# Making w_out's sums for seven-product pairs two pairs at a time, all in batch 1's first half

## The chip, the cores and the metric

One core of one Trainium2 chip runs the whole program. The core has five engines that are told apart here: TensorE (PE, matrix products; its weight loads are listed as PEld), VectorE (DVE), ScalarE (ACT), GpSimd (POOL) and SyncE (SP), which issues the DMA transfers here. The metric is device microseconds of one execution of the kernel. Three runs of the kernel before took 710.82, 713.46 and 713.57 us.

## The reference

Inputs are q, k, v of 8 batches x 8 heads x 576 rows x 64, packed queries p of 32 rows, a w_in of 512 x 2048 and a w_out of 2048 x 512. Cut to what matters:

```
def sm_attn(qq, kk, vv):
    s = scale * np.matmul(qq, kk.transpose(0, 1, 3, 2))
    s = s - np.max(s, axis=-1, keepdims=True)
    a = np.exp(s)
    a = a / (np.sum(a, axis=-1, keepdims=True) + 1e-09)
    return np.matmul(a, vv)
p_packed = sm_attn(p, k, v)
out = sm_attn(q, p_packed, p_packed)          # 8 x 8 x 576 x 64

x = out, heads put side by side               # 4608 tokens x 512
h = x @ w_in                                  # 4608 x 2048
g = h * np.clip(h + 3.0, 0.0, 6.0) / 6.0
return g @ w_out                              # 4608 x 512
```

The packed result of 32 rows serves as keys and as values of the second attention. Behind the attention stand two large products with a gate between them.

## The kernel before, in words

The work goes batch by batch. Batch 0 has its order written out by hand (a long list of steps) and is not touched. For batches 1 to 7, while the two large products of batch b run, the attention of batch b + 1 is made a piece at a time between them.

A batch's 576 tokens are done in two halves (c = 0 and 1; of 320 and 256 tokens in one order or the other, the odd 64 tokens of two neighbouring batches being joined in an "edge" tile). A half walks over the 2048 columns of w_in in 16 steps of 128 columns, f = 0 to 15. In each step `first_product` (L929) makes h for 128 columns: 12 matmuls a step on the halves `a_hi`, `a_lo` and `m_hi`, `m_lo`, since every float32 operand is split into a high part and a low part and three products (high by high, high by low, low by high) are summed. `m` is w_in already multiplied with the packed keys, so that the second attention's result needn't be formed: u_m, L350, makes it from w_in a quarter (512 columns) at a time, which is why w_in is needed again in every batch. It is kept in DRAM as `w_kept` (written at batch 1's step 0, L1376, four transfers of 1 MB) and fetched back as `w_again` (L1380).

`gate_into` makes the gate: a ReLU on ACT (L940) and a multiply with a minimum on DVE (L941). Then g is split: ACT casts the high part (L946), POOL or DVE subtracts for the low part (L947). The second products (L969) of a step are queued and come two steps later, or, for pairs, one pair later, so that the gate and the split have time.

A single step costs the second product 6 matmuls of 512 columns (two blocks of 128 tokens by three products). A *pair* takes two steps f, f + 1 at once as a 2 x 2 block product with seven instead of eight block products: 21 matmuls of 256 columns in place of 12 of 512. For that the left sides are added and subtracted on DVE for each pair and each half (L1196, L1204, L1209: S1 to S4), and the right sides, four sums T1 to T4 of w_out's blocks B11, B12, B21 and B22, are made once for a pair by `combine` and used in all batches from then on. T3 takes the place of B12 in w_out itself. T1, T2 and T4 go to slots in the three buffers that w_in's second to fourth quarter leave. There are four such slots for six pairs (`PAIRS`): two pairs' blocks are kept in DRAM (`t_kept`, L1100) and two fetched again (`fetch_t`, L1104) in each half.

Batch 1's first half runs 16 single steps (`moe`), while `combine` makes the sums of pairs 0 to 3 at the steps that `TURN` names. POOL adds the high and the low part of T3's and B22's blocks (L1071), DVE does the rest (L1082 to L1095), ACT and DVE split each result (L1075, L1076), all in operations of 256 columns. Batch 1's second half has four pairs (`FIRST_PAIRS`) and eight single steps, and the sums of pairs 4 and 5 are made in its last five steps. All later halves have six pairs and four singles; the first half of a batch takes the pairs in reverse.

What runs between the products is set by `fill`, once a step: `LATE` for batch 1's own u_m, `TURN` for `combine`, `FETCHES`, and `STAGES`, which says from which of the 32 steps of a batch the loading, the packed attention and the second attention's softmax (u_s2, L494 to L524, on DVE for the most part) of the next batch start, and how many pieces a step takes. A scheduler then places the instructions of each engine in one fixed order; each engine works through its own list strictly in that order and waits where an operand isn't there.

## Time and profile before

| | |
|---|---|
| three runs | 710.82, 713.46, 713.57 us |
| the profiled execution's own time | 714.05 us, its span 712.2 us, mean granted clock 0.99 |
| PE, PEld busy | 691.6, 594.8 us |
| DVE, ACT, POOL busy | 532.0, 428.6, 353.6 us |
| batch 1's first half (from its first `ps_hh` product) | 119.96 to 169.63 us |
| batch 1's second half | 169.63 to 213.07 us |
| batch 2's first half | 213.07 to 251.11 us |
| the same half of batch 4 | 381.83 to 417.92 us |

The span is the stretch of one execution that the profiler recorded; its times are microseconds from the span's start. A row of a group gives line, engine, operation, what is written and read, the shapes and the count, then busy time, the mean of one in ns, and the idle time of the engine ahead of it with what ended it. A row of the chain gives start, length and what it consists of. A row of a timeline gives start, duration, engine, line, operation, and in brackets how long the engine was idle before and what released it. A row of windows gives a stretch, its length, and of PE, PEld, DVE, ACT and POOL the busy time and the number of records, then the clock granted to TensorE (1.00 is full speed), the share that the DMA engines were busy, and GB/s.

### The profile page before, as it was taken

The page shows a single profiled execution, that of the slowest core. Times are in us where ns is not written, and L with a number is a line of the kernel's source. Part 1 is how long each engine was busy: PE and PEld are TensorE (multiplying, and loading weights), DVE is VectorE, ACT ScalarE, POOL GpSimd, SP SyncE. Part 2 cuts the span into 40 slices and gives each one's busy share as a digit, 9 for nine tenths or more (in the row PEclk, how much of TensorE's full clock was granted, in tenths as well). Part 3 has the DMA queues.
Part 4 walks back from the last instruction along what each step waited for, and adds up shares of the span by engine and source line. Part 5 has one row for each costly group of instructions (what it writes and reads, how often), then busy time and mean ns, then how long its engine had stood idle before and what let it go on. Part 6 is the DMA issues. An engine that isn't in the chain of part 4 may idle for free.

```text
span 712.2 us, 16078 instructions
## 1 busy us (share of the span) xinstructions
PE 691.6 (97%) x5906; PEld 594.8 (84%) x5906; DVE 532.0 (75%) x1169; ACT 428.6 (60%) x1013; POOL 353.6 (50%) x539
## 2 busy tenths in 40 slices
PE   6699999999999999999999999999999999999997
PEld 5477876888878888899798988899888898889997
DVE  3888788587899779786598867888488876975453
ACT  4798876556565655665366655657356564756453
POOL 1456642555353454465353534556354444547553
PEclk9799999999999999999999999999999999999999
DMA  9969953855327756474554657375543745331030
GB/s 264 338 153 273 217 149 119 258 152 117 108 106 196 169 137 209 118 175 76 129 193 136 161 116 222 109 154 139 130 164 119 165 122 178 119 134 46 30 105 29
DMA packets 199102, 107.48 MB, mean 151 GB/s; under 512 B 173424, under 2 KB 185200, under 8 KB 195440
## 3 DMA queue, kind: packets, MB, share of 16 engines
q1 hardware_dynamic: 198480, 106.26, 54.4%
q8 instruction: 46, 0.75, 0.5%
q14 instruction: 32, 0.26, 0.1%
q10 hardware_dynamic: 544, 0.20, 0.1%
HBM read 89.65 MB, written 16.78 MB: 149 GB/s over the span
## 4 chain that ended last, share of the span: by engine, by line
PE 87%; DVE 6%; DMA 4%; ACT 1%; issue 1%; SPq 1%; POOL 0%; DVEq 0%; ACTq 0%
PE acc L969 48%; PE ps_hh L929 23%; PE ps L350 5%; PE ps_h L607 4%; PE ps L969 2%; PE ps L470 1%; DMA nat<-in_k_dram 1%; DMA wt<-t_kept 1%; PE ps L440 1%; DVE tr L555 1%; PE ps_t L678 1%; DMA k_nat<-in_k_dram 1%; SPq L294 1%; PE ps L273 1%; DMA w_again<-w_kept 1%
## 5 line engine op out<-in xcount | busy, mean ns | idle before, releaser
L929 PE MATMUL ps_hh<-a_hi,m_hi 128*128 128x320 f32 (+1 forms) x448 | 134.8, 301 | 1.5 <-PE acc L969 0.8
L929 PE MATMUL ps_hh<-a_lo,m_hi 128*128 128x320 f32 (+1 forms) x448 | 133.9, 299 | 0.0
L929 PE MATMUL ps_hh<-a_hi,m_lo 128*128 128x320 f32 (+1 forms) x448 | 133.4, 298 | 0.0
L941 DVE SCALAR_TENSOR_TENSOR t<-t,ps_hh 128x320 f32<-128x320 f32 (+1 forms) x148 | 66.0, 446 | 58.9 <-ACT t L940 58.3
L947 POOL TENSOR_TENSOR gf<-tb,gf 128x256 fp32r<-128x256 f32 x76 | 64.6, 851 | 87.4 <-ACT gf L946 56.2
L969 PE MATMUL acc<-wo_hi,g 128*128 128x512 f32 x288 | 103.1, 401 | 0.0
L940 ACT ACTIVATE t<-ps_hh,three 128x320 f32<-128x320 f32 (+1 forms) x148 | 73.9, 500 | 35.0 <-PE ps_hh L929 29.0
L929 PEld LDWEIGHTS ps_hh<-a_hi,m_hi 128*128 128x128 f32 x448 | 85.2, 190 | 10.0 <-issue 3.0
L929 PEld LDWEIGHTS ps_hh<-a_lo,m_hi 128*128 128x128 f32 x448 | 85.2, 190 | 6.5 <-issue 3.5
L929 PEld LDWEIGHTS ps_hh<-a_hi,m_lo 128*128 128x128 f32 x448 | 85.1, 190 | 2.9 <-issue 2.5
L947 POOL TENSOR_TENSOR g<-t,g 128x256 fp32r<-128x256 f32 x72 | 55.7, 775 | 45.4 <-ACT g L946 23.3
L969 PE MATMUL acc<-wt,ga 128*128 128x256 f32 x456 | 74.6, 284 | 0.2
L969 PE MATMUL acc<-wo_hi,ge 128*128 128x256 f32 x304 | 71.5, 286 | 0.2
L947 POOL TENSOR_TENSOR ga<-t,ga 128x256 fp32r<-128x256 f32 x76 | 62.4, 821 | 13.6 <-ACT ga L946 12.3
L969 PEld LDWEIGHTS acc<-wt,ga 128*128 128x128 f32 x456 | 63.0, 190 | 3.3 <-ACT ga L946 1.7
L969 PEld LDWEIGHTS acc<-wo_hi,g 128*128 128x128 f32 x288 | 53.0, 189 | 13.7 <-POOL g L947 3.0
L969 PEld LDWEIGHTS acc<-wo_hi,ge 128*128 128x128 f32 x304 | 52.9, 189 | 8.6 <-ACT t L940 2.1
L965 POOL COPY bnd<-t 128x64 f32<-128x64 f32 x76 | 23.0, 302 | 70.2 <-DVE t L941 64.4
L969 PE MATMUL acc<-wo_lo,g 128*128 128x512 f32 x144 | 56.9, 395 | 0.0
L555 DVE STREAM_TRANSPOSE tr<-nat 128x576 f32<-128x576 f32 x56 | 42.3, 764 | 17.4 <-DMA nat<-in_q_dram 11.8
L940 ACT ACTIVATE tb<-ps_hh,three 128x256 f32<-128x256 f32 (+1 forms) x76 | 37.8, 498 | 19.5 <-PE ps_hh L929 18.5
L946 ACT CAST g<-t 128x256 fp32r<-128x256 f32 x72 | 29.2, 407 | 33.6 <-DVE t L941 33.0
(222 smaller groups left out, 1840.4 us busy)
## 6 DMA issues: line engine op xcount, KB each, us to landing
w_again<-w_kept SPq DMA_DIRECT2D x24, 1024.0 KB, 4.9
wt<-t_kept SPq DMA_DIRECT2D x24, 768.0 KB, 5.4
out_dram<-osb SPq DMA_DIRECT2D x33, 256.0 KB, 2.5
nat<-in_k_dram SPq DMA_DIRECT2D x112, 72.0 KB, 3.2
nat<-in_q_dram SPq DMA_DIRECT2D x112, 72.0 KB, 2.7
raw_in<-in_moe_w_in_dram SPq DMA_DIRECT2D x10, 512.0 KB, 5.2
raw_out<-in_moe_w_out_dram SPq DMA_DIRECT2D x10, 512.0 KB, 5.3
w_kept<-w_in_sb SPq DMA_DIRECT2D x4, 1024.0 KB, 9.4
```

The source lines that it names most:

```text
L273: nc.tensor.matmul(banks[x][NPK * a:NPK * a + NPK, :n * P], state["pp"][half, NPAIR * x + a], cols[half, :, a], start=True, stop=True,)
L294: nc.sync.dma_start(out=t[r:r + 32], in_=src[b, 2 * a + h, :, 32 * c:32 * c + 32].rearrange("(t i) j -> i t j", i=32),)
L350: nc.tensor.matmul(pair[x][NPK * a:NPK * a + NPK, :n], rows[half, a], c, start=True, stop=True)
L555: nc.vector.transpose(out=t, in_=state.pop(("nat", which, b, a)))
L607: nc.tensor.matmul(h[:, hf, :HS], mm[:, g, fs], aa[:, hf * HS:(hf + 1) * HS], start=(g == 0 and i == 0), stop=(g == NG - 1 and i == 2),)
L929: state["first"] = nc.tensor.matmul(h[:, :n], mm[:, g, fs], aa[:, t0:t0 + n], start=(g == 0 and i == 0), stop=(g == NG - 1 and i == 2),)
L940: state["relu"] = nc.scalar.activation(out=t[:, :n], in_=h, func=AF.Relu, bias=three)
L941: state["gate"] = nc.vector.scalar_tensor_tensor(out=t[:, :n], in0=t[:, :n], scalar=6.0, in1=h, op0=ALU.min, op1=ALU.mult)
L946: nc.scalar.copy(out=hi, in_=x)
L947: engine.tensor_sub(out=lo, in0=x, in1=hi.bitcast(F32))
L965: nc.gpsimd.tensor_copy(out=bnd[:, f, side * REM:side * REM + REM], in_=t[:, boff:boff + REM])
L969: nc.tensor.matmul(out, lhs[x], rhs[y], start=first and i == 0, stop=last and i == 2, skip_group_check=True)
```

## The change

`combine(j)` now makes the sums of two pairs, 2j and 2j + 1, at a time, in operations of 512 columns where the blocks of the two lie in one tile. It works in a tile `turning` with four places x, u, v and y, which takes the buffer (`w_in0`) of w_in's first quarter. POOL now adds high and low part of T3, B22 and B11; DVE makes the differences and splits. `TURN` gives three such chains, pairs 4 and 5 first (j = 2, their y in two tiles `wy`), then 0 and 1, then 2 and 3, all between steps 4 and 15 of batch 1's first half. T1, T2 and T4 have a tile each, so that a store and a fetch of a pair or two consist of three transfers. Batch 1's second half then has six pairs and four singles as all later halves, with the fetches that belong to them. Two things go with it: the packed attention for batch 2 starts at step 10 instead of 6, and the lower part of batch 2's v, whose buffer is also `w_in0`, is loaded at step 13.

```diff
@@ -20,15 +20,13 @@
 
 
 
-STAGES = (((0, 1), (6, 2), (19, 2)), ((0, 1), (10, 2), (19, 1)))
+STAGES = (((0, 1), (10, 2), (19, 2)), ((0, 1), (10, 2), (19, 1)))
 
 
 LATE = (3, 2, 1, 2, 1)
 PAIRS = 6
-FIRST_PAIRS = 4
 TURN = (
-    (5, 5, 6, 6, 7, 7, 7), (7, 8, 8, 9, 9, 9, 10), (10, 10, 11, 11, 12, 12, 12), (13, 13, 13, 14, 14, 15, 15),
-    (27, 27, 28, 28, 28, 29, 29), (29, 29, 30, 30, 30, 31, 31),
+    (2, (4, 6, 7, 7, 8, 8, 9, 14)), (0, (9, 9, 10, 10, 11, 11, 12)), (1, (12, 12, 13, 13, 14, 14, 15)),
 )
...
@@ -573,7 +571,8 @@
         yield
         turn("k", b, 3)
         load("q", b, 1)
-        load_v_low(b)
+        if b != 2:
+            load_v_low(b)
         yield
...
         cols = slice(0, H2) if name in ("B11", "B21") else slice(H2, DM)
         return [wo_at(part, f)[:, cols] for part in ("hi", "lo")]
 
+    def combine(j):
+
+        if not slots:
+            slots.extend(wr.tile([P, 4, 2, H2], F32R, name=f"wt{k}", tag=f"w_in{k}") for k in range(1, 4))
+            for i in range(PAIRS):
+                for k, name in enumerate(("T1", "T2", "T4")):
+                    blocks[i, name] = [slots[k][:, i % 4, x] for x in range(2)]
+            t = wr.tile([P, 4, 2, H2], F32, name="turning", tag="w_in0")
+            turning.extend(t[:, n] for n in range(4))
+        last = j == 2
+        at = 0 if last else 2 * j
+        x, u, v, y = turning
+        if last:
+            y = [xp.tile([P, W + P], F32, name="wy", tag="tb")[:, :H2] for _ in range(2)]
+        whole = slice(0, 2)
+
+        def t3(n):
+            return y[n] if last else y[:, n]
+
+        def rows(name, wide=True):
+            f = 4 * j + (name in ("B21", "B22"))
+            cols = slice(0, H2) if name in ("B11", "B21") else slice(H2, DM)
+            late = f >= EARLY
+            if wide and late == (f + 2 >= EARLY):
+                f -= EARLY * late
+                return [(whole, *(wo[late][part][:, f:f + 3:2, cols] for part in ("hi", "lo")))]
+            return [(n, *block(2 * j + n, name)) for n in range(2)]
+
+        def summed(dst, name, wide=True):
+            for n, hi, lo in rows(name, wide):
+                nc.gpsimd.tensor_tensor(out=dst(n), in0=hi.bitcast(F32), in1=lo.bitcast(F32), op=ALU.add)
+
+        def split(hi, lo, made):
             nc.scalar.copy(out=hi, in_=made)
             nc.vector.tensor_sub(out=lo, in0=made, in1=hi.bitcast(F32))
 
+        def kept(k, made):
+            split(*(slots[k][:, at:at + 2, part] for part in range(2)), made)
+
+        def kept_t3():
+            for n, hi, lo in rows("T3", not last):
+                split(hi, lo, t3(n))
+
+        spans = (0, 1) if last else (whole,)
+        summed(lambda n: x[:, n], "T3")
+        yield
+        summed(t3, "B22", not last)
+        yield
+        summed(lambda n: u[:, n], "B11")
+        yield
+        for n in spans:
+            nc.vector.tensor_sub(out=t3(n), in0=x[:, n], in1=t3(n))
+        nc.vector.tensor_sub(out=x, in0=x, in1=u)
+        kept(0, x)
+        yield
+        for n in spans:
+            nc.vector.tensor_sub(out=u[:, n], in0=u[:, n], in1=t3(n))
+        for n, hi, lo in rows("B21"):
+            nc.vector.tensor_sub(out=v[:, n], in0=hi.bitcast(F32), in1=u[:, n])
+            nc.vector.tensor_add(out=v[:, n], in0=v[:, n], in1=lo.bitcast(F32))
+        yield
+        kept(1, u)
+        if not last:
+            kept_t3()
+        yield
+        kept(2, v)
+        if j != 1:
+            for k in range(3):
+                nc.sync.dma_start(
+                    out=t_kept[k, :, j:j + 2].rearrange("p i m -> p (i m)"),
+                    in_=slots[k].bitcast(F32)[:, at:at + 2].rearrange("p i x m -> p (i x m)"),
+                )
+        yield
+        if last:
+            kept_t3()
+            yield
 
     def fetch_t(i):
+        for k in range(3):
+            nc.sync.dma_start(
+                out=slots[k].bitcast(F32)[:, i % 4].rearrange("p x m -> p (x m)"),
+                in_=t_kept[k, :, i % 4 + i // 4 * 2],
+            )
 
     def moe_pairs(b, c, fill):
 
+        pairs = list(range(PAIRS))
         if c == 0:
             pairs.reverse()
         n_pairs = len(pairs)
@@ -1370,7 +1404,7 @@
     xp = ctx.enter_context(tc.tile_pool(name="xp", bufs=2))
     dram = ctx.enter_context(tc.tile_pool(name="dram", bufs=1, space=bass.MemoryType.DRAM))
     w_kept = dram.tile([NCH, P, FPC * DM], F32, name="w_kept")
-    t_kept = dram.tile([PAIRS - 2, P, 3 * DM], F32, name="t_kept")
+    t_kept = dram.tile([3, P, PAIRS - 2, DM], F32, name="t_kept")
 
     def keep_w_in(n):
         nc.sync.dma_start(out=w_kept[n], in_=w_in_sb[n].rearrange("p f a e -> p (f a e)"))
@@ -1393,13 +1427,15 @@
         ahead = coarse(ahead)
         if b == 1:
             late = coarse(part for n in range(1, NCH) for part in u_m(1, n))
-            turned = [combine(i) for i in range(PAIRS)]
+            turned = [combine(j) for j, _ in TURN]
         else:
             late = coarse(u_m(b, NCH - 1))
         soon = first_quarters(b + 1) if more else iter(())
 
         def fill(c, f):
             s = c * NF + f
+            if (b, s) == (1, 13):
+                load_v_low(2)
             with behind_gates():
                 if b == 1:
                     for _ in range(LATE[s] if s < len(LATE) else 0):
@@ -1408,12 +1444,13 @@
                         with tc.issue_after(state["stored"].ins):
                             for n in range(NCH):
                                 keep_w_in(n)
-                    for i in range(PAIRS):
-                        for _ in range(TURN[i].count(s)):
-                            next(turned[i], None)
+                    for chain, (_, when) in zip(turned, TURN):
+                        for _ in range(when.count(s)):
+                            next(chain, None)
                 else:
                     if s > 0:
                         next(late, None)
+                if (b, c) > (1, 0):
                     for at, i in FETCHES[c]:
                         if f == at:
                             fetch_t(i)
@@ -1430,7 +1467,7 @@
         for c in range(2):
             if (b, c) == (1, 0):
                 moe(b, (c,), lambda f, c=c: fill(c, f))
-                rest(*turned[:FIRST_PAIRS])
+                rest(*turned[:2])
                 roles.extend((3, 0, 1, 2))
             else:
                 moe_pairs(b, c, lambda f, c=c: fill(c, f))
```

Lines of the changed kernel lie one to thirty off those of the kernel before: `gate_into` and the splits are L940 and L946 where they were L941 and L947, first and second products L928 and L968, u_m L348, POOL's sums L1086, the pairs' left sides L1230, L1238 and L1243.

Where instructions move, the order on three engines is shown for two places in the program. On POOL, at the start of batch 1's first half: `g` with a number is the low part of a step's gate (1622 is step 0's, 1661 step 1's), `bnd` the copy of the odd 64 tokens. Before:

```order
L947 TENSOR_TENSOR g_1622<-t,g_1622 128x256
L965 COPY bnd<-t 128x64
L947 TENSOR_TENSOR g_1661<-t,g_1661 128x256
L947 TENSOR_TENSOR edge<-bnd,edge 128x256
L965 COPY bnd<-t 128x64
L947 TENSOR_TENSOR g_1687<-t,g_1687 128x256
L965 COPY bnd<-t 128x64
L947 TENSOR_TENSOR g_1733<-t,g_1733 128x256
```

With the change:

```order
L946 TENSOR_TENSOR g_1622<-t,g_1622 128x256
L964 COPY bnd<-t 128x64
L1086 TENSOR_TENSOR turning<-wo_hi,wo_lo 128x512 x3
L946 TENSOR_TENSOR g_1661<-t,g_1661 128x256
L946 TENSOR_TENSOR edge<-bnd,edge 128x256
L964 COPY bnd<-t 128x64
L946 TENSOR_TENSOR g_1687<-t,g_1687 128x256
L964 COPY bnd<-t 128x64
L946 TENSOR_TENSOR g_1733<-t,g_1733 128x256
```

Three adds of 512 columns into `turning` now stand ahead of step 1's low part.

On PE, in the same place, where step 1's products with the low part (the two rows `acc<-wo_hi,g_1661` together) follow. Before:

```order
L969 MATMUL acc<-wo_hi,edge 128x512
L969 MATMUL acc<-wo_lo,edge 128x512
L350 MATMUL ps_1700<-w_in_sb_1073,pps 32x512 x8
L969 MATMUL acc<-wo_hi,g_1661 128x512 x2
L929 MATMUL ps_hh<-a_hi,m_hi 128x320
L929 MATMUL ps_hh<-a_lo,m_hi 128x320
L929 MATMUL ps_hh<-a_hi,m_lo 128x320
```

With the change:

```order
L968 MATMUL acc<-wo_hi,edge 128x512
L968 MATMUL acc<-wo_lo,edge 128x512
L348 MATMUL ps_1700<-w_in_sb_1073,pps 32x512 x8
L928 MATMUL ps_hh<-a_hi,m_hi 128x320
L928 MATMUL ps_hh<-a_lo,m_hi 128x320
L928 MATMUL ps_hh<-a_hi,m_lo 128x320
L928 MATMUL ps_hh<-a_hi,m_hi 128x320
L928 MATMUL ps_hh<-a_lo,m_hi 128x320
L928 MATMUL ps_hh<-a_hi,m_lo 128x320
L968 MATMUL acc<-wo_hi,g_1661 128x512 x2
L968 MATMUL acc<-wo_hi,g_1687 128x512
```

Six first products of a later step now stand ahead of the two that read `g_1661`'s low part.

On DVE, in batch 1's second half, from the gate of its seventh or eighth step on: `z`, `den` and `at` belong to batch 2's attention, `ge` is the low part of a pair's first step, L1196, L1204 and L1209 (L1230, L1238 and L1243) make a pair's left sides. Before:

```order
L941 SCALAR_TENSOR_TENSOR tb<-tb,ps_hh 128x256
L518 STREAM_TRANSPOSE at<-z 128x576
L947 TENSOR_TENSOR ge<-t,ge 128x256
L513 RECIPROCAL den_2514<-den_2514 128x18
L1204 TENSOR_TENSOR t<-t,tb 128x2x128
L515 TENSOR_TENSOR z<-z,den_2514 128x576
L524 TENSOR_TENSOR a_lo<-at,a_hi 128x576
L1209 TENSOR_TENSOR tb<-tb,t 128x128
L539 TENSOR_TENSOR m_lo<-ps_2533,m_hi 128x512
L941 SCALAR_TENSOR_TENSOR t<-t,ps_hh 128x256
```

With the change:

```order
L516 STREAM_TRANSPOSE at<-z 128x576
L940 SCALAR_TENSOR_TENSOR t<-t,ps_hh 128x256
L940 SCALAR_TENSOR_TENSOR tb<-tb,ps_hh 128x256
L516 STREAM_TRANSPOSE at<-z 128x576
L1243 TENSOR_TENSOR tb<-tb,t 128x128
L1230 TENSOR_TENSOR t<-t 128x128
L522 TENSOR_TENSOR a_lo<-at,a_hi 128x576
L1238 TENSOR_TENSOR t<-t,tb 128x2x128
L522 TENSOR_TENSOR a_lo<-at,a_hi 128x576
L946 TENSOR_TENSOR ge<-t,ge 128x256
L1243 TENSOR_TENSOR tb<-tb,t 128x128
```

Both transposes `at` and both `a_lo` now stand ahead of the `ge` that is shown.

36 lines of the change are left out of this document (1 added, 35 removed).

## The prediction

> **What bounds the kernel now.** I read the page's busy shares first, then the chain of waits, then tables of windows over the steady part, over batch 1's two halves and over batch 2's first half, and last single rows on each engine in the places that the change touches.
>
> ```profile
> PE 691.6 (97%) x5906; PEld 594.8 (84%) x5906; DVE 532.0 (75%) x1169; ACT 428.6 (60%) x1013; POOL 353.6 (50%) x539
> PE 87%; DVE 6%; DMA 4%; ACT 1%; issue 1%; SPq 1%; POOL 0%; DVEq 0%; ACTq 0%
> ```
>
> TensorE (PE) is busy for 97% of the span and carries 87% of the chain. VectorE (DVE) at 75% and GpSimd (POOL) at 50% have room on average, but an average over 712 us hides where they are short. The windows show that (each row: stretch, its length, PE, PEld, DVE, ACT, POOL busy with counts, granted clock, DMA share, GB/s):
>
> ```profile
> 239.00:322.00 83.00, 83.00 (x749) 73.13 (x750) 65.54 (x148) 49.33 (x120) 43.08 (x77) 1.00 0.57 155
> 119.96:169.63 49.67, 49.67 (x375) 40.23 (x376) 36.43 (x80) 28.55 (x69) 27.73 (x45) 1.00 0.65 187
> 169.63:213.07 43.44, 42.48 (x316) 34.48 (x315) 38.04 (x82) 24.62 (x64) 18.93 (x26) 0.96 0.43 125
> 192.65:196.06 3.41, 2.45 (x14) 1.63 (x13) 3.41 (x8) 1.49 (x5) 0.94 (x3) 1.00 0.00 0
> 196.06:199.48 3.42, 3.42 (x16) 3.25 (x17) 3.42 (x8) 2.76 (x7) 3.12 (x5) 0.50 0.01 2
> ```
>
> In the steady part PE never stops: only fewer or shorter matmuls can gain there. Batch 1's first half is the second row, its second half the third, and that one is different: DVE is busy 38.04 of 43.44 us, PE loses time, and in one stretch of 3.4 us (last row) the granted clock is 0.50. These places, all within batch 1 and the start of batch 2, are where the change can gain or lose. I price it there, against the profiled execution's own 714.05 us; the runs shown have the median 713.46, so the result is shifted by -0.6 at the end.
>
> **Part 1, fewer products.** Batch 1's second half makes six pairs and four singles instead of four and eight. A pair, and a single step, on PE:
>
> ```profile
> 243.56 2.52 PE acc L969 x21
> 208.50 1.40 PE acc L969 x6
> 242.12 1.44 PE ps_hh L929 x12
> ```
>
> 21 products of 256 columns take 2.52 us, so 0.12 each; two singles take 2.8. I take 0.25 saved per pair (some single rows are 1.38): **-0.5 us** for two pairs. The first products are the same in both, 0.12 each at 256 columns.
>
> **Part 2, the sums on POOL at the start of batch 1.** Three adds of 512 columns into `turning` now stand on POOL ahead of step 1's low part `g`. `turning` takes over the buffer of w_in's first quarter, so the first add waits until that quarter's copy to DRAM (`w_kept`) has landed; `g` and everything behind it on POOL waits too, and PE's products of step 1 wait for `g`. The copy's issue and landing, POOL's rows at that place, and PE's where it needs the result:
>
> ```profile
> 120.75 4.12 SPq L1376 DMA_DIRECT2D w_kept<-w_in_sb  x4
> DMA to landing us min/median/max: 6.5/9.4/11.6
> 124.32 0.24 POOL L965 COPY bnd<-t 128x64 f32<-128x64 f32 x1 [0.85 <-DVE t L941]
> 125.28 0.74 POOL L947 TENSOR_TENSOR g<-t,g 128x256 fp32r<-128x256 f32 x1 [0.72 <-ACT g L946]
> 177.31 0.46 POOL L947 TENSOR_TENSOR ga<-tb,ga 128x128 fp32r<-128x128 f32 x1
> 128.64 0.72 PE L969 MATMUL acc<-wo_hi,g 128*128 128x512 f32 x2
> ```
>
> The first of the four copies is issued at 120.75 and lands 6.5 us later at the earliest, at 127.25; POOL is at the add from 124.56. A 512-column add isn't in the trace. 128 columns take 0.46 and 256 take 0.74, which continued by the same 0.28 per 128 columns gives an estimate of 1.30; the bounds are 0.74 (no longer than 256) and 1.66 (twice the 0.83 that L1071's adds take on average, below). Three adds end at 127.25 + 3.9 = 131.15, the low part at 131.9. PE meets the product that needs it after step 4's first products, where the rows of before stand at about 129.5 (the changed order puts six more L929 matmuls of 320 columns ahead of the two at 128.64; by 0.12 for 256, 0.15 each). So PE waits **+2.4 us**. Low bound: adds of 0.74 give 0.7. High bound: if the copy lands after the median 9.4 us, 5.3. I take the middle because the first copy issued has the queue to itself. Behind this, POOL is late by 6 us, but it is busy only 27.73 of the 49.67 us of the half (window rows), so I let it catch up before another product meets it. That cover is needed: the change gives POOL a further 9 sums of two pairs where it had 2 of 256 columns a pair, about 6.5 us more over the half.
>
> **Part 3, the clock behind that wait.** The last two window rows above show what a wait of this size did: 14 products of 0.12 are 1.7 us of the 3.41, so PE was without work for 1.7 us, spread over several gaps, and in the next 3.42 us the granted clock is 0.50, with only 16 matmuls. A window at half speed costs 1.7. I read from this that a loss of 1.7 in a window is enough, and charge **+1.7** for the 2.4 of part 2 (bounds 0 and 1.7).
> The Trainium skill ("TensorE: Matmul & The Clock Gate", "What's actually happening") says that the clock halves after at least one idle window of 3413 ns. The trace agrees on the window's length, but the gate closed here after a window in which PE had 2.45 us of records. By the page's rule nothing would be charged; that is a rival below.
>
> **Part 4, six pairs in batch 1's second half.** Here POOL's and DVE's sums of T1..T4 for pairs 4 and 5 leave, but DVE has, between step 21's gate and the `ge` low parts of the pairs behind it, the same attention work in another order. DVE and PE now, and the costs of the kinds (groups between 178 and 196.5):
>
> ```profile
> 178.12 0.42 DVE L941 SCALAR_TENSOR_TENSOR tb<-tb,ps_hh 128x256 f32<-128x256 f32 x1
> 195.22 0.28 DVE L1209 TENSOR_TENSOR tb<-tb,t 128x128 f32<-128x128 f32 x1
> 195.88 0.45 PE L969 MATMUL acc<-wo_hi,ga 128*128 128x256 f32 x1 [0.65 <-ACT ga L946]
> L947 DVE TENSOR_TENSOR ge<-t,ge 128x256 fp32r<-128x256 f32 x3 | 1.8, 591 | 1.1 <-ACT ge L946 1.1
> L1204 DVE TENSOR_TENSOR t<-t,tb 128x256 f32<-128x256 f32 x3 | 1.7, 579 | 0.0
> L494 DVE STREAM_TRANSPOSE z<-ps 128x288 f32<-128x288 f32 x4 | 1.7, 457 | 0.0
> L504 DVE TENSOR_TENSOR z<-z,mx 128x576 f32<-128x576 f32 x2 | 1.5, 765 | 0.0
> L515 DVE TENSOR_TENSOR z<-z,den 128x576 f32<-128x576 f32 x2 | 1.5, 744 | 0.0
> L509 DVE TENSOR_REDUCE den<-z 128x18 f32<-128x576 f32 x2 | 1.5, 742 | 0.0
> L502 DVE TENSOR_REDUCE mx<-z 128x18 f32<-128x576 f32 x2 | 1.5, 728 | 0.0
> L941 DVE SCALAR_TENSOR_TENSOR t<-t,ps_hh 128x256 f32<-128x256 f32 x3 | 1.2, 411 | 0.8 <-ACT t L940 0.8
> L539 DVE TENSOR_TENSOR m_lo<-ps,m_hi 128x512 fp32r<-128x512 f32 x1 | 0.7, 677 | 0.0
> ```
>
> DVE works from 178.12 to 195.5 with hardly a gap, and PE at 195.88 waits for what comes out of that line: DVE is the bound there. In the changed order DVE makes, from step 21's gate to the `ge` of pair 4, five gates (2.05), three L1204 (1.74), three `ge` (1.77), two L1209 (0.55), two differences like them (0.64), four `z` transposes (1.83), two each of the maximum, the subtraction, the sum and the division (1.46 + 1.53 + 1.48 + 1.49), two reciprocals (0.5) and two `m_lo` (1.36): 16.4 us, and 0.5 ahead of them for the ReLU. PE reaches the same point after 75 products and 36 first products of 0.12 and three pieces of u_m:
>
> ```profile
> 240.20 0.65 PE ps L350 x16
> 200.51 1.02 PE ps L350 x16
> ```
>
> 9.0 + 4.3 + 2 x 0.65 + 1.02 = 15.6, up to 16.2 with the small gaps that the rows show between groups; so it waits 0.7. For pair 5's `ge` DVE needs another 6.8 (a pair's own work by the same rows, and the rest of the attention's), PE 5.2 (about 43 products and first products of 0.12), so it waits another 1.6, 2.3 in all. The same count of before's rows gives 2.2 where the window shows 1.7, so I scale and take 1.8: **+0.1 us**. But these waits stand in two or three windows of the clock instead of one, each below the 1.7 that a window lost at 192.65, so I count the half-clock window of before as gone: **-1.7** (bounds -1.7 and 0).
>
> **Part 5, batch 2's first half.** Before, pairs 4 and 5 are summed in batch 1's last steps, and their chain is late into batch 2:
>
> ```profile
> 220.53 0.34 DVE wt L1076
> 224.60 0.38 PE L929 MATMUL ps_hh<-a_hi,m_hi 128*128 128x256 f32 x1 [0.42 <-DVE tb L941]
> 238.86 0.50 PE L969 MATMUL acc<-wt,gf 128*128 128x256 f32 x2 [0.26 <-DMA wt<-t_kept]
> 213.07:251.11 38.04, 37.15 (x304) 32.87 (x303) 31.37 (x75) 21.98 (x59) 15.49 (x22) 1.00 0.74 176
> 381.83:417.92 36.09, 36.09 (x304) 32.50 (x303) 28.36 (x68) 21.40 (x56) 15.02 (x22) 1.00 0.66 160
> ```
>
> The half takes 38.04 us, the same half of batch 4 36.09 with as many matmuls, so 1.95 is lost. DVE has 3 us more to do (31.37 against 28.36; the sums' L1076 at 220.53 is part of it), which the change takes away; what stays is the wait for the fetch at 238.86, some 0.4 with its gap. **-1.5 us** (bounds -1.95 and 0).
>
> **Part 6, what is hidden.** The sums of batch 1's first half on DVE are half as many operations of twice the width; the busy time I count equal, since the elements are (four pairs before, six now, but T3, B22 and B11 of all of them on POOL), and DVE is busy 36.43 of 49.67 there. The six stores and the loads of v for batch 2, which move to step 13 because their buffer is taken, find the DMA engines at a share of 0.65; v is first read at step 18, after some 15 us, so nothing (late: up to 1.5). Each later fetch is three transfers of 256 KB instead of one of 768 KB:
>
> ```profile
> wt<-t_kept SPq DMA_DIRECT2D x24, 768.0 KB, 5.4
> ```
>
> The bytes are the same and land in about the same time; the first block that PE reads of a reversed pair (T4) is now issued third. The one wait for a fetch above, 0.26, shows that a margin is small in batch 2; in the steady row (239 to 322) none is waited for, so I take nothing (the bound is rival D).
>
> The sum: -0.5 + 2.4 + 1.7 + 0.1 - 1.7 - 1.5 = **+0.5 us**, 714.55 in a profiled execution, and about **714.0** as the median. That is no change: about 0.5%, 3.6 us, is what a measurement of this kernel can tell from none.
>
> **Rivals.**
> A, *the clock reacts only to a window that is idle throughout.* Then part 3's 1.7 falls away, while a wait in part 4 stays without it too: -0.5 + 2.4 + 0.1 - 1.7 - 1.5 = -1.2, about 712.3. Against it: the row of 196.06 follows a window with 2.45 us of PE records. For it: it is one event. This is the page's rule; the verdict would still be "no change".
> B, faster: *batch 1's second half becomes like the later ones.* They run six pairs without a stall (239 to 322: 83.00 of 83.00), with the same attention work beside them. Then both the 1.7 us of waits and the 1.7 of the clock go (-3.4), and the adds on POOL are at their lower bound (+0.7 and no clock): -0.5 + 0.7 - 3.4 - 1.5 = -4.7, about 708.8. Against it: batch 1 makes the u_m of its own batch late, and DVE holds 31.67 of 35 us there. It decides where DVE's 16.9 comes below PE's 16.2.
> C, slower: *DVE's sums slow down beside POOL's.* DVE's operation with two operands in SBUF takes twice as long in places where POOL works on an add:
>
> ```profile
> 178.57 0.43 DVE L1204 TENSOR_TENSOR t<-t,tb 128x256 f32<-128x256 f32 x1
> 185.70 0.96 DVE L1204 TENSOR_TENSOR t<-t,tb 128x256 f32<-128x256 f32 x1
> 185.63 0.75 POOL L947 TENSOR_TENSOR gf<-tb,gf 128x256 fp32r<-128x256 f32 x1 [2.81 <-ACT gf L946]
> L1071 POOL TENSOR_TENSOR wx<-wo_hi,wo_lo 128x256 f32<-128x256 f32 x10 | 8.3, 830 | 4.7 <-DVE wo_lo L1076 3.4 <-DVE wt L1076 1.1
> ```
>
> With six pairs each half has two more of each such operation; at 0.96 and twice L1209's 0.28 the burst of part 4 grows by about 3 us, all of it into PE's wait, and the clock then falls as before. -0.5 + 2.4 + 1.7 + 0.1 + 3.0 + 0 - 1.5 = +5.2, about 718.6. It decides from about 2 us more on DVE. Against it: POOL loses its own sums of pairs 4 and 5 there.
> The Trainium skill ("SBUF — State Buffer", "Who interferes with whom") says that VectorE and GpSimd share a pair of ports under an exclusive lock, which speaks for this rival wherever the wider adds lie beside DVE's work; the pair of L1204 rows agrees.
> D, slower: *T4, fetched third, lands late.* The three parts share one queue; if each takes a third of the 5.4 us and the last has 1 us of overhead on top, the halves that start with reversed pairs (the first of batches 2 to 7, six) lose up to 0.6 each beyond what they have now: 0.5 + 3.6 = +4.1, so 717.6. Against it: the row of before has all 768 KB landed as one.
>
> **How the numbers follow.** The forecast 0.36, A 0.20, B 0.23, C 0.14, D 0.07. Forecast and A lie within 0.5%, of which I leave some to each side for sizes; so faster by over 0.5% 0.24, within 0.5% 0.54, slower 0.22. The range goes from B's 708.8 to C's 718.6, 709.0 to 718.5, and leaves out the halves of B and C beyond; the likeliest case's own range, with part 2 at its bounds and the other terms as taken, is 712.3 to 716.9.
>
> **What would show it.** Part 2: after 120 us a first `turning` add on POOL that ends with a DMA wait, and PE idle 2 to 3 us before an `acc<-wo_hi,g` at about 129 to 132. Part 3: a window at clock 0.5 right behind it. Part 4: the second half of batch 1 without clock 0.5, with gaps before products of `ge`; a half 2.2 us shorter than 43.44 agrees. Part 5: batch 2's first half near 36.5 us. Wrong I am if the first half of batch 1 is no longer than its 49.67 us, if the second half runs without gaps (B), if L1204's rows there are mostly 0.9 and its waits 4 us or more (C), or if `wt` fetches end PE's waits in later batches (D).

## The result, and the profile after

The changed kernel takes 717.21 us, the median of ten runs (713.72 to 718.99), beside 712.84 us for the kernel before (ten runs, 710.6 to 714.75). The ratio is 1.0058, with a 95% interval of 1.0036 to 1.0081: by this ratio 4.1 us slower (2.6 to 5.8). That is in the forecast range of 709.0 to 718.5, but above the forecast 714.0, above 716.9, where the likeliest case's own range ended, and, if barely, past the 0.5% within which it was to lie. All ratios, here and below, leave out three runs in a slow state (837.21 us of the kernel before, 949.69 and 2312.96 us of two variants). The profiled execution took 717.95 us with a span of 716.2; before it was 714.05 and 712.2.

The page of the changed kernel, the busy shares and the chain:

```profile
PE 692.2 (97%) x5924; PEld 596.0 (83%) x5924; DVE 527.3 (74%) x1144; ACT 427.5 (60%) x1007; POOL 359.4 (50%) x542
PE 82%; DVE 7%; DMA 4%; ACT 3%; issue 2%; SPq 1%; POOL 1%; DVEq 0%; ACTq 0%; POOLq 0%
```

Over the whole span nothing seems to have happened: DVE has 5 us less to do, POOL 6 more. The chain says more, since PE's share in it fell from 87% to 82%. The windows of the halves tell where (columns as before: length, then PE, PEld, DVE, ACT, POOL, granted clock, DMA share, GB/s); the last two rows are the window of the clock in which PE waits, and the next one, both taken 0.14 us behind the clock's own steps at 130.30 and 133.71, hence 0.98 and 0.52:

```profile
121.27:174.79 53.52, 50.88 (x295) 40.07 (x296) 39.33 (x70) 27.35 (x65) 35.08 (x46) 0.97 0.61 187
174.79:217.31 42.52, 40.84 (x413) 34.77 (x414) 31.35 (x73) 25.54 (x64) 18.78 (x28) 1.00 0.59 167
217.31:254.48 37.17, 36.39 (x304) 32.82 (x303) 30.10 (x70) 22.15 (x57) 15.20 (x22) 1.00 0.68 161
130.44:133.85 3.41, 1.57 (x9) 1.18 (x8) 1.07 (x2) 1.22 (x3) 3.41 (x6) 0.98 0.96 363
133.85:137.26 3.41, 3.41 (x11) 2.73 (x10) 1.28 (x3) 1.70 (x5) 3.06 (x6) 0.52 0.83 137
```

Batch 1's first half is 3.85 us longer (49.67 before), its second half 0.92 shorter (43.44), batch 2's first half 0.87 shorter (38.04). The first half lost still more than its length says, because 1.3 us of matmuls (the packed attention's products with v, L468) moved from it to the second half. Another 1.31 us lie ahead of all this: batch 1 begins at 121.27 instead of 119.96. PE, POOL and SP at the places that the prediction named:

```profile
128.40 3.80 POOL L1086 TENSOR_TENSOR turning<-wo_hi,wo_lo 128x512 f32<-128x512 f32 x3 [2.53 <-DMA w_kept<-w_in_sb]
132.16 0.72 POOL L946 TENSOR_TENSOR g<-t,g 128x256 fp32r<-128x256 f32 x1
132.93 1.00 PE L968 MATMUL acc<-wo_hi,g 128*128 128x512 f32 x3 [1.83 <-POOL g L946]
DMA to landing us min/median/max: 6.2/9.1/11.5
```

POOL stands 2.53 us until the copy `w_kept` has landed (6.2 us after its issue, the last row's minimum), the three adds take 3.80, so 1.27 each, and PE waits 2.0 us at 132.93, where part 2 of the prediction has its wait of 2.4. (The row's idle time is 1.83; 2.0 is how much later the matmul starts than at the usual distance from the one ahead of it, since a matmul's record is longer than that distance.) The half-clock window behind it, a stretch of 3.41 us at a granted clock of 0.50, is there too. Then there are waits that were not forecast in this form:

```profile
166.07 0.50 PE L968 MATMUL acc<-wo_hi,edge 128*128 128x512 f32 x1 [0.18 <-POOL edge L946]
174.79 0.39 PE L928 MATMUL ps_hh<-a_hi,m_hi 128*128 128x256 f32 x1 [0.62 <-DVE t L940]
179.09 1.27 SPq L407 DMA_DIRECT2D v_nat<-in_v_dram  x2
182.33 0.32 PE L468 MATMUL ps<-v_nat,et 64*32 64x64 f32 x8 [0.18 <-DMA v_nat<-in_v_dram]
205.26 1.09 PE L348 MATMUL ps<-w_again,pps 64*32 64x512 f32 x16 [1.49 <-DVE at L516]
231.33 0.38 PE L928 MATMUL ps_hh<-a_hi,m_hi 128*128 128x256 f32 x1 [0.78 <-DVE t L940]
409.50 0.50 PE L968 MATMUL acc<-wt,gf 128*128 128x256 f32 x2 [0.45 <-DMA wt<-t_kept]
```

Measured by lateness again, the six matmuls cost 0.35, 0.78, 0.39, 1.65, 0.94 and 0.60 us; the third row is the issue of the loads of v that the matmul at 182.33 waits for. The profile says that DVE's transpose `at` ended the wait at 205.26, but L348 doesn't read `at`: it reads `w_again`. That transfer was issued at 197.95 and took 7.2 us, where the median of these loads is 4.9:

```profile
197.95 8.81 SPq L1414 DMA_DIRECT2D w_again<-w_kept  x2
DMA to landing us min/median/max: 7.2/7.2/7.2
```

197.95 + 7.2 = 205.15, 0.1 us before the matmul. Before the change the same transfer was issued at 187.13 and needed by 200.51. It comes later because its buffer is the one that `turning`, then v, then the first fetched quarter hold in turn, and v is loaded when `turning` has been read.

### The profile page after: what moved, and what is told of

Same layout as the page of the kernel before. It is cut to its first block, busy times and chain, and to the rows that moved or that the text cites. A ratio compares the mean times of both kernels' runs of the same rounds, so it can differ in the third digit from the quotient of the medians.

```text
span 716.2 us, 16218 instructions
## 1 busy us (share of the span) xinstructions
PE 692.2 (97%) x5924; PEld 596.0 (83%) x5924; DVE 527.3 (74%) x1144; ACT 427.5 (60%) x1007; POOL 359.4 (50%) x542
## 4 chain that ended last, share of the span: by engine, by line
PE 82%; DVE 7%; DMA 4%; ACT 3%; issue 2%; SPq 1%; POOL 1%; DVEq 0%; ACTq 0%; POOLq 0%
PE acc L968 45%; PE ps_hh L928 22%; PE ps L348 5%; PE ps_h L606 3%; PE ps L968 2%; PE ps L468 1%; DMA w_kept<-w_in_sb 1%; DVE wt L1090 1%; DMA wt<-t_kept 1%; DMA raw_in<-in_moe_w_in_dram 1%; PE ps_t L677 1%; PE ps L271 1%; PE ps L438 1%; DMA k_nat<-in_k_dram 1%; DVE tr L553 1%
## 5 line engine op out<-in xcount | busy, mean ns | idle before, releaser
L928 PE MATMUL ps_hh<-a_hi,m_hi 128*128 128x320 f32 (+1 forms) x448 | 134.3, 300 | 2.2 <-DVE t L940 1.4
L928 PE MATMUL ps_hh<-a_lo,m_hi 128*128 128x320 f32 (+1 forms) x448 | 133.5, 298 | 0.0
L928 PE MATMUL ps_hh<-a_hi,m_lo 128*128 128x320 f32 (+1 forms) x448 | 133.0, 297 | 0.0
L940 DVE SCALAR_TENSOR_TENSOR t<-t,ps_hh 128x320 f32<-128x320 f32 (+1 forms) x146 | 65.3, 447 | 68.1 <-ACT t L939 65.9
L946 POOL TENSOR_TENSOR gf<-tb,gf 128x256 fp32r<-128x256 f32 x78 | 65.8, 845 | 90.1 <-ACT gf L945 57.3
L968 PE MATMUL acc<-wo_hi,g 128*128 128x512 f32 x272 | 97.6, 403 | 1.8 <-POOL g L946 1.8
L928 PEld LDWEIGHTS ps_hh<-a_hi,m_hi 128*128 128x128 f32 x448 | 84.8, 189 | 10.4 <-issue 3.8
L928 PEld LDWEIGHTS ps_hh<-a_lo,m_hi 128*128 128x128 f32 x448 | 84.8, 189 | 6.8 <-issue 4.0
L928 PEld LDWEIGHTS ps_hh<-a_hi,m_lo 128*128 128x128 f32 x448 | 84.6, 189 | 3.8 <-issue 3.4
L968 PE MATMUL acc<-wt,ga 128*128 128x256 f32 x468 | 76.3, 284 | 0.0
L968 PE MATMUL acc<-wo_hi,ge 128*128 128x256 f32 x312 | 73.3, 285 | 0.0
L946 POOL TENSOR_TENSOR g<-t,g 128x256 fp32r<-128x256 f32 x68 | 52.1, 766 | 40.6 <-ACT g L945 24.3
L946 POOL TENSOR_TENSOR ga<-t,ga 128x256 fp32r<-128x256 f32 x78 | 63.8, 818 | 15.7 <-ACT ga L945 15.4
L968 PEld LDWEIGHTS acc<-wt,ga 128*128 128x128 f32 x468 | 64.7, 190 | 2.9 <-ACT ga L945 0.9
L968 PEld LDWEIGHTS acc<-wo_hi,g 128*128 128x128 f32 x272 | 49.8, 189 | 14.1 <-POOL g L946 5.3
L968 PEld LDWEIGHTS acc<-wo_hi,ge 128*128 128x128 f32 x312 | 54.5, 190 | 7.7 <-DVE t L940 2.5
L968 PE MATMUL acc<-wo_lo,g 128*128 128x512 f32 x136 | 54.0, 397 | 0.0
L553 DVE STREAM_TRANSPOSE tr<-nat 128x576 f32<-128x576 f32 x56 | 42.4, 764 | 13.7 <-DMA nat<-in_q_dram 10.9
L939 ACT ACTIVATE tb<-ps_hh,three 128x256 f32<-128x256 f32 (+1 forms) x78 | 38.8, 498 | 20.5 <-PE ps_hh L928 19.4
L946 POOL TENSOR_TENSOR edge<-bnd,edge 128x256 fp32r<-128x256 f32 (+1 forms) x50 | 33.2, 670 | 32.4 <-ACT edge L945 32.3
```

Source lines behind the costliest of these rows:

```text
L553: nc.vector.transpose(out=t, in_=state.pop(("nat", which, b, a)))
L928: state["first"] = nc.tensor.matmul(h[:, :n], mm[:, g, fs], aa[:, t0:t0 + n], start=(g == 0 and i == 0), stop=(g == NG - 1 and i == 2),)
L939: state["relu"] = nc.scalar.activation(out=t[:, :n], in_=h, func=AF.Relu, bias=three)
L940: state["gate"] = nc.vector.scalar_tensor_tensor(out=t[:, :n], in0=t[:, :n], scalar=6.0, in1=h, op0=ALU.min, op1=ALU.mult)
L946: engine.tensor_sub(out=lo, in0=x, in1=hi.bitcast(F32))
L968: nc.tensor.matmul(out, lhs[x], rhs[y], start=first and i == 0, stop=last and i == 2, skip_group_check=True)
```

## The experiments

Theory 1 was that the early loss (the wait at 132.93 and the half-clock window behind it) comes from POOL's wide adds waiting for the copy of w_in; theory 2 that the wait at 205.26 is the fetch `w_again`; theory 3 that DVE, late at the end of the half, causes the one at 174.79. Against each stood the rival that another engine sets the pace, so that a gain in one place comes back in the next.

### The sums queued behind the low part of the step before

```diff
-                            next(chain, None)
+                            with tc.issue_after(state["low"].ins):
+                                next(chain, None)
```

(`state["low"]` is POOL's last low part; this queues POOL's adds behind it.)

> The changed kernel with one thing different: each sum on POOL is queued behind the low part g of the step before it, so the three adds into turning no longer stand ahead of step 1's low part. Theory 1 (the adds' wait for w_kept costs PE 2.0 us and then a window of the half clock 1.7): the wait at about 133 us and the window at 0.5 behind it are gone, batch 1's first half is 3 to 3.7 us shorter than 53.5, the kernel about 713.5 to 714.2 us against 717.2. Rival (DVE is the bound of the whole half, so sums that come later end later): the 2.0 us come back as waits at the end of the half, 0.8 us there now becoming 3 or more, and the kernel stays within 1.5 us of 717.2, except for the clock.

Measured: 716.32 us, ratio 1.0039 (1.0022 to 1.0055), not the expected 713.5 to 714.2. The early wait and its half-clock window are gone, and the first half is 50.24 us. But the time came back. The windows of the two halves, and then PE in them:

```profile
118.65:168.89 50.24, 49.13 (x296) 39.14 (x297) 36.13 (x65) 26.67 (x63) 36.23 (x49) 1.00 0.66 201
168.89:215.34 46.45, 43.65 (x415) 36.21 (x414) 35.08 (x78) 26.64 (x67) 20.00 (x28) 0.96 0.52 150
160.92 0.55 PE L438 MATMUL ps<-ident,e 128*128 128x128 f32 x3 [0.80 <-DVE turning L1117]
171.77 0.39 PE L928 MATMUL ps_hh<-a_hi,m_hi 128*128 128x256 f32 x1 [0.63 <-DVE t L940]
177.49 0.32 PE L468 MATMUL ps<-v_nat,et 128*32 128x64 f32 x8 [0.45 <-DMA v_nat<-in_v_dram]
```

The sums end later on DVE (`turning` at 160.92), v is loaded later, the attention follows, and in the second half, now 46.45 us, another half-clock window falls (clock 0.96 over the half). By lateness the waits for v grew from 0.4 to 2.4 us. So the adds do cause the early loss, and yet taking them later gains only 0.9 us of 717.21, which the intervals of the two ratios do not tell from nothing. The rival is half right: the chain from the copy over the sums to v's load has little slack.

### Two of the three adds left ahead

The chain of pairs 4 and 5 stays as it is, only the other two chains are queued behind low parts.

> The changed kernel with two of the three adds left ahead of step 1's low part, the sums of the other pairs queued behind low parts. Two adds of 1.27 us end at 128.3 + 2.5 = 130.8, the low part at 131.5 (in the times of the changed kernel's profile), so PE waits 0.6 to 0.8 us instead of 2.0. Theory 1 with a clock that needs more than about 1.7 us of loss in a window: no window at 0.5, about 714 us. Rival (any stop of PE at that place lowers the clock): a window at 0.5 behind a wait of 0.7, about 715.8 us.

Measured: 716.02 us, ratio 1.0053 (1.0021 to 1.0084), where 714 was expected, the runs widely spread (713.77 to 722.38). POOL and PE in it:

```profile
125.55 2.56 POOL L1088 TENSOR_TENSOR turning<-wo_hi,wo_lo 128x512 f32<-128x512 f32 x2 [2.52 <-DMA w_kept<-w_in_sb]
128.07 0.72 POOL L946 TENSOR_TENSOR g<-t,g 128x256 fp32r<-128x256 f32 x1
128.85 0.50 PE L970 MATMUL acc<-wo_hi,g 128*128 128x512 f32 x1 [0.58 <-POOL g L946]
```

One add less, 1.28 us, shortens the wait to 0.7, and no half-clock window follows. That settles the size of part 2; the time of the whole kernel settles nothing, since the spread is larger than the effect.

### u_m one step later

```diff
+            if (b, n) == (2, NCH - 3):
+                yield
             yield from coarse(u_m(b, n))
```

> The changed kernel with the u_m piece of w_in's second fetched quarter taken one step later in batch 1's second half (two steps in PE's order). Theory 2 (PE's 1.65 us before u_m at 205.26 waits for w_again, issued at 197.95 and landed at 205.13, because its buffer is now free 11 us later than before): the wait is gone or under 0.3 us, nothing else waits instead, about 715.6 us. Rival (PE waits for DVE's transpose at, which the profile names as what ended the wait, so DVE's line of work is the bound there): the wait moves to the next products of a pair, the second half stays at 42.5 us and the kernel at 717.2.

Measured: 715.5 us, ratio 1.0024 (1.0005 to 1.0043), where theory 2 said 715.6. The second half is 40.74 us instead of 42.52, but 1.0 us of that is another piece of u_m, 16 products, which now stands behind its end, at 213.97. Three windows of the clock, and PE in both places of interest:

```profile
127.29:130.70 3.41, 3.02 (x27) 1.47 (x25) 0.69 (x1) 0.59 (x1) 2.94 (x3) 1.00 1.03 416
130.70:134.11 3.41, 1.82 (x8) 1.52 (x9) 1.17 (x2) 1.68 (x4) 3.41 (x7) 1.00 1.06 308
134.11:137.52 3.41, 3.41 (x19) 2.94 (x18) 1.17 (x3) 1.65 (x5) 2.31 (x5) 1.00 0.65 106
132.29 0.73 PE L968 MATMUL acc<-wo_hi,g 128*128 128x512 f32 x2 [1.98 <-POOL g L946]
202.33 0.50 PE L968 MATMUL acc<-wo_hi,ge 128*128 128x256 f32 x2 [0.55 <-DVE ge L946]
```

The wait for `w_again` is gone; what remains is one for pair 4's `ge`, 0.7 us by its lateness, the place that part 4 had computed. The expectation had said that nothing else would wait, so that the time fits better than the theory. It was the transfer and not DVE that bound at 205.26, and DVE's line of work stands 1 us behind it. The other four rows show what was not looked for. Here PE waits 2.14 us for POOL's adds as well, and yet no half-clock window follows. The windows of the clock lie on a fixed grid of 3.41 us in an execution; its phase follows from the execution's own half-clock windows. In the changed kernel's profile the whole wait (130.9 to 132.9) lay in one window (130.30 to 133.71); here a boundary, at 130.72, cuts it into 0.57 and 1.57.

### Three adds in the kernel before

```diff
+                    if s == 2:
+                        spare = wr.tile([P, 4, 2, H2], F32, name="spare", tag="w_in0")
+                        for n in range(3):
+                            nc.gpsimd.tensor_tensor(out=spare[:, n], in0=..., in1=..., op=ALU.add)
```

> The kernel before, with three adds of 512 columns on POOL into an unused tile that takes over the buffer of w_in's first quarter, in the same place as in the changed kernel (ahead of step 1's low part). Their results are used by nothing. Theory 1: the same 2.0 us wait of PE at about 131.5 and a window of the clock at 0.5 behind it, 3.7 us in all, so about 716.5 against 712.84. Rival (the loss belongs to the rest of the change): within 1 us of 712.84.

Measured: 715.02 us, ratio 1.0028 (1.001 to 1.0047): 2 us where 3.7 were expected, the wait without the clock. The adds and PE in it, and the two halves:

```profile
126.25 3.82 POOL L1414 TENSOR_TENSOR spare<-wo_hi,wo_lo 128x512 f32<-128x512 f32 x3 [2.13 <-DMA w_kept<-w_in_sb]
130.81 0.50 PE L969 MATMUL acc<-wo_hi,g 128*128 128x512 f32 x1 [1.46 <-POOL g L947]
119.53:170.92 51.39, 49.93 (x376) 40.33 (x377) 37.53 (x81) 28.75 (x70) 32.57 (x49) 1.00 0.63 181
170.92:213.47 42.55, 41.32 (x317) 33.13 (x316) 36.32 (x77) 23.93 (x60) 17.62 (x25) 1.00 0.42 127
```

The adds alone, with nothing else of the change, make PE wait 1.6 us; the first half is 1.7 longer than before, and no half-clock window follows. The second half is nearly that of the kernel before, with four pairs and the same stalls of DVE around 195, but it has no half-clock window in this execution: a boundary, at 197.07, cuts the stalls, and 1.6 us of them lie ahead of it. The half-clock window of the kernel before, which part 4 counted as gained, was thus not fixed to that place.

### The first copy alone

The copies of w_in's other three quarters are issued behind the first loads of batch 2's next block of k.

> The changed kernel with only the order of transfers different: of w_in's four copies to DRAM the first goes alone, the other three behind the first loads of batch 2's next block of k. The orders on PE, DVE and POOL stay. Theory 1 (POOL's first add waits for the landing of that copy, which takes 6.2 us beside the three others): it lands after 4.7 to 5 us, the adds start 1.2 to 1.5 us earlier against the first product of the half, PE's wait falls from 2.0 to 0.5 to 0.8 us, and batch 1's first half, without a half-clock window, is near 50.8 us where e3_um_later, which has the wait and no such window, has 52.06. Rival (the wait stands on POOL's own 3.8 us of wide adds, not on the copy): the wait stays at 1.5 us or more.

Measured: 719.53 us, ratio 1.0082 (1.0055 to 1.0108). The expectation was wrong. The landing of these four copies, POOL and PE:

```profile
DMA to landing us min/median/max: 4.3/6.4/8.8
127.97 3.80 POOL L1086 TENSOR_TENSOR turning<-wo_hi,wo_lo 128x512 f32<-128x512 f32 x3 [2.81 <-DMA w_kept<-w_in_sb]
132.50 1.22 PE L968 MATMUL acc<-wo_hi,g 128*128 128x512 f32 x2 [2.12 <-POOL g L946]
```

The first copy was issued at 121.34 and POOL's add starts at 127.97: with no other copy issued behind it for 5.9 us it lands no sooner, 6.5 us after its issue. So the three others do not delay it. What does is open: the first of the three, issued at 127.24, lands after 4.3 us, and two stores of the output stand 0.9 us ahead of the first copy, which no run takes away. In this execution a second half-clock window, from 207.2, follows a wait for `w_again` of 1.8 us.

### T3's split later

```diff
-    (2, (4, 6, 7, 7, 8, 8, 9, 14)), ...
+    (2, (4, 6, 7, 7, 8, 8, 9, 16)), ...
-                rest(*turned[:2])
+                rest(turned[1])
```

> The changed kernel with the last piece of the sums of pairs 4 and 5 (the split of T3: two casts on ACT, two subtractions of 256 columns on DVE, 0.76 us) moved from step 14 to step 16. Theory 3 (at the end of batch 1's first half DVE is late with the gate of the last step, and PE waits 0.78 us at 174.79 and 0.35 us at 166.07): the wait ahead of the second half's first product falls by 0.4 to 0.8 us; 716.6 against 717.2, so at the edge of what can be told. Rival (DVE only catches up later): the same time comes back within the next four steps.

Measured: 716.82 us, ratio 1.0054 (1.0035 to 1.0072), as expected at the edge of what can be told. The wait ahead of the second half's first product fell from 0.78 to 0.45 us, idle before it 0.29:

```profile
174.79 0.38 PE L928 MATMUL ps_hh<-a_hi,m_hi 128*128 128x256 f32 x1 [0.29 <-DVE t L940]
```

DVE is late there, and half of the 0.76 us that were moved shows up. But the wait at 166, which theory 3 had named too, stayed (0.33 for 0.35 us), and the waits for v behind it grew from 0.4 to 0.9 us, so the rival, that the time comes back, isn't excluded.

### A first combination

The first copy alone, u_m later, T3's split later, and T4 fetched first (`for k in (2, 0, 1)` in `fetch_t`).

> The changed kernel with four things different: the first copy of w_in alone, u_m's piece of the second fetched quarter one step later, T3's split at step 16, and T4 fetched first of a pair's three blocks. The theories add up to -1.5 - 1.65 - 0.5 and, by fewer windows of the half clock, about -1 from 717.2: 712.5 us, the same as before within what can be told. Rival (the chain of sums, v's load and the packed attention sets the pace, so that what one place gains comes back at the next): 714 or more.

Measured: 714.61 us, ratio 1.0023 (1.0005 to 1.0041), 2.1 us above what was expected. The wait for POOL was still there (2.19 us) with a half-clock window behind it, as the run before this one explains.

### The first copy ahead of batch 0's stores

```diff
+                        with tc.issue_after(state["load"].ins):
+                            keep_w_in(0)
                         with tc.issue_after(state["stored"].ins):
-                            for n in range(NCH):
+                            for n in range(1, NCH):
                                 keep_w_in(n)
```

> The changed kernel with one thing different: the copy of w_in's first quarter to DRAM is issued behind batch 0's last weight load instead of behind its stores, some 20 us earlier; the other three copies stay. POOL's three wide adds then stand ahead of step 0's low part, in the 9.5 us in which POOL was idle. Theory 1 (PE's wait of 2.0 to 2.3 us and the half-clock window that can follow come from the adds' wait for this copy, and nothing else): no wait of PE at 131 to 133, no window at 0.5 behind it, batch 1's first half 50.0 to 50.3 us (52.06 without such a window, less 2.0); the kernel about 714 us. Rival (the chain of sums sets the pace, or, as when the sums were queued behind low parts, what is gained early comes back at v's load and the packed attention): the second half grows by 1.5 us or more, the kernel stays at 715.5 or above.

Measured: 714.63 us, ratio 1.0033 (1.0015 to 1.0051). The wait at 131 to 133 is gone, but the expected 50.0 to 50.3 us became 51.44, and the loss now lies at the very beginning.

### The second combination

The same with u_m later, T3's split later and T4 first.

> The same, with u_m's piece of the second fetched quarter one step later, T3's split at step 16 and T4 fetched first. Theories 1 to 3 add up to -2.0 (wait), -1.65 (w_again), about -0.3 (T3) and about -1 to -1.5 for half-clock windows that no longer follow: 712 us, within 0.5% of the kernel before, at best 711. Rival (the gains come back): 714 or more, as the earlier combination, which still had PE's wait behind the copy, at 714.6.

Measured: 711.89 us, ratio 0.9992 (0.9972 to 1.0013), where 712 was expected. Its beginning shows what happens in both. DVE, POOL and PE, around 119:

```profile
118.40 3.80 POOL L1086 TENSOR_TENSOR turning<-wo_hi,wo_lo 128x512 f32<-128x512 f32 x3 [5.03 <-PE ps L348]
118.44 1.33 DVE L1311 COPY bnd<-t 128x64 f32<-128x64 f32 x1
119.69 1.87 DVE L537 TENSOR_TENSOR m_lo<-ps,m_hi 128x512 fp32r<-128x512 f32 x3
121.78 0.39 PE L928 MATMUL ps_hh<-a_hi,m_hi 128*128 128x320 f32 x1 [1.94 <-issue]
```

and the same copy in the changed kernel, where POOL is idle beside it:

```profile
119.08 0.19 DVE L1311 COPY bnd<-t 128x64 f32<-128x64 f32 x1
```

DVE's copy of 128x64 takes 1.33 us instead of 0.19 because it begins 0.04 us after POOL's add, and it ends 0.1 us after the first of the three adds does (1.27 each). It waited for one whole add. `m_lo` behind it is 1.14 us late, and with it the first product of batch 1; a half-clock window follows. The Trainium skill ("SBUF — State Buffer", "Who interferes with whom") says that where a DVE instruction uses the pair of ports that it shares with GpSimd, whoever issues first holds the pair for the whole instruction; the 1.33 and 0.19 agree, though no row tells whether this copy uses that pair.

### The adds behind step 1's edge

In the last combination POOL's adds are put back to where the changed kernel has them, behind step 1's copy `bnd`; the early copy of w_in's first quarter stays.

> The last combination (early copy of w_in's first quarter, u_m one step later, T3's split at step 16, T4 fetched first) with POOL's three wide adds put back behind the copy bnd of step 1. In the combination they stood ahead of step 0's work; there DVE's copy L1311 of 128x64, beside POOL's first add, took 1.33 us instead of 0.19, batch 1's first product came 1.14 us late (2.10 instead of 0.96), and a window of the half clock followed. Theory 4 (that lateness is DVE held up by POOL's add, and with the copy of w_in landed early the adds cost nothing at their old place): first product 0.96 as before, adds from 125.9 to 129.7, step 1's low part at 130.4, before PE needs it at 130.9, so no wait over 0.3 us and no window at 0.5 between 120 and 140; batch 1's first half 49 to 49.5 us, the kernel 709.5 to 710.5. Rival (the time comes back at the end of the half or at v's load): the first half 50.5 or more, the kernel at 711.5 or above.

Measured: 711.18 us, ratio 0.997 (0.9954 to 0.9987). POOL, and batch 1's two halves and batch 2's first:

```profile
125.23 0.24 POOL L964 COPY bnd<-t 128x64 f32<-128x64 f32 x1 [0.86 <-DVE t L940]
125.42 3.83 POOL L1086 TENSOR_TENSOR turning<-wo_hi,wo_lo 128x512 f32<-128x512 f32 x3
129.20 0.73 POOL L946 TENSOR_TENSOR g<-t,g 128x256 fp32r<-128x256 f32 x1
120.86:170.07 49.21, 48.80 (x295) 38.92 (x296) 39.34 (x69) 27.20 (x65) 34.54 (x46) 1.00 0.61 181
170.07:211.35 41.28, 40.54 (x397) 34.75 (x398) 31.10 (x73) 24.66 (x62) 18.67 (x27) 1.00 0.61 173
211.35:248.46 37.11, 37.11 (x320) 32.86 (x319) 29.20 (x72) 22.33 (x58) 15.57 (x23) 1.00 0.69 161
```

The adds start 0.2 us after `bnd` with no wait for a transfer, and no product waits for them. The first half is 49.21 us (expected 49 to 49.5), 4.3 less than in the changed kernel. Theory 4 holds. This version is faster than both kernels, by 0.3% than the one before (0.13 to 0.46); the changed one stands at 1.0058 against the same kernel. The time is 0.7 us above the end of what was expected.

## Why the prediction was right, and where it was off

The time lies in the range because the range reached up to rival C's time, and C's mechanism didn't come about: that is luck. Of the terms, parts 2 and 3 and the direction of part 5 came as forecast; the 3.4 us by which the profiled execution is above the forecast 714.55 come mainly from part 6, put at nothing, and from 1.3 us ahead of batch 1.

**The bound (right).** PE is the bound, and all of the difference lies in batch 1 and the start of batch 2, apart from two pieces. The 1.31 us ahead of batch 1 are the execution's own: the orders there are the same, the two traces run level from 45 to 90 us, and then weights for batch 0 land later; of the ten variants the eight without a new wait at that place begin batch 1 anywhere from 118.44 to 121.57. And 0.6 us stand at 409.50, below.

**Part 1, fewer products (-0.5).** Not measured by itself. It is too small to be separated from the waits in the same half.

**Part 2, POOL's wait (+2.4).** Right in mechanism and near in size: 2.0 us, and 1.6 to 2.3 in five other kernels that have it. Its reason for the landing time, that the first copy has the queue to itself, isn't borne out: two stores of the output are issued just ahead of it (at 119.87 in the kernel before). The add of 512 columns took 1.27 against an estimate of 1.30, the copy landed after 6.2 against 6.5. Two adds gave 0.7, a copy issued earlier gave none. Also right was that POOL catches up before another product meets that lateness.

**Part 3, the clock (+1.7).** It fell in this execution, as forecast. But it was priced as a consequence of the wait alone, and the runs show that it depends on where the wait lies. Waits of 2.0 to 2.3 us were followed by a half-clock window where the whole of it, or at least some 1.9 us, lay within one window (the changed kernel, the first copy alone, T3 later, the first combination), and not where a boundary cut it (u_m later) or where it was 1.6 us (three adds in the kernel before). So what was off is the price: 1.7 us times a probability, not 1.7, and four such executions of five are too few to give the probability. The loss that was held to be enough was too low as well: by lateness the window at 192.65 of the kernel before lost 1.97 us, not 1.7. The timed runs don't give the average either. The granted clock over the span is 0.9881 in the mean of the changed kernel's ten runs and 0.9898 in that of the 94 listed for the kernel before beside the experiments; 2 x (1 - clock) x time gives 17.1 us at half clock against 14.6. But the profiled executions also run at half clock near their beginning, for 10.2 us in the kernel before (from 25.4), 13.7 in the changed one (from 24.5) and 17.1 in the last variant (from 19.4), and these stretches alone differ by more.

**Part 4, the second half (+0.1 and -1.7).** The wait came, 1.65 us against 1.8, but its cause was another: not DVE's line of work but `w_again`, whose buffer comes free 11 us later. So it is luck that the sizes are near. The prediction looked at that buffer only as far as v's load. With the transfer out of the way, the wait for pair 4's `ge` appeared, 0.7 us as computed; the 1.6 computed for pair 5 did not. The -1.7 for the clock was right for this pair of profiles and too much for the average, since the kernel with three adds, with the same stalls, didn't have that window.

**Part 5, batch 2's first half (-1.5).** It measured -0.87. The late sums are gone, but a gate behind DVE's transposes of k is late in their place (231.33, 0.94 us). In the last variant, with the transfers of batch 1 in time, this half has no wait (PE 37.11 of 37.11, with 16 products of u_m, 1.0 us, more than in the changed kernel).

**Part 6, what is hidden (0).** This is the term that was most wrong: 1.27 us in the last steps of the first half (0.78 at 174.79, where DVE still has two splits of the sums to make ahead of the gate; 0.35 at 166.07, where POOL's `edge` is late behind its own sums; 0.14 at 162.81), and 0.39 where v is late. The prediction compared DVE's busy time with the half's length, but the sums of two pairs stand in few long pieces in its last steps; and it allowed v a landing some 15 us before its use, where the loads were issued from 177.03 on and the last of them landed at 182.28, 0.05 us before the matmul at 182.33. These and the wait for `w_again` belong to one chain, copy, sums, v, attention, fetch, and the first experiment shows that it has little slack: the sums shifted back, the waits for v grew to 2.4 us.

Worked from these, with part 1's -0.5 taken over unmeasured, the profile's difference is 1.3 (batch 0) + 2.0 + 1.7 (parts 2 and 3) + 1.3 + 0.4 (part 6) - 0.5 + 1.65 - 1.7 - 1.7 (parts 1 and 4: the wait that came, the 1.7 us of waits and the half-clock window that went) - 0.9 + 0.6 = +4.1 against 3.9 measured.

**The rivals.** A, that the clock reacts only to a window that is idle throughout, falls: the window from 130.44 has 1.57 us of PE records, and the next is at half clock. Of the Trainium skill's rule ("TensorE: Matmul & The Clock Gate", "What's actually happening") the window's length and its free-running grid agree; an entirely idle window isn't needed here. B, six pairs without a stall, came nearly true only in the last variant, where PE is idle for 0.74 of the second half's 41.28 us. C, DVE slowed by POOL's adds, didn't come about in the second half: all six of L1238 (L1204 before) took 0.41 to 0.43 us there; that POOL holds DVE up is shown at another place, at 118.44 of the second combination. D, T4 landing late, is open in size: 0.6 us at 409.50, and in two of the six other variants that fetch T4 third the same half is 1.5 us longer, while in the three with T4 first it is 35.98 each time. That is suggestive, but no run changed it alone.
